# A fused attention, Fourier and MLP kernel whose tile scheduler orders the engines by its detailed timeline model

## The chip, the core and the metric

The kernel runs on one core of one Trainium2 chip. The metric is the device time of one execution in microseconds. Before the change the median of three runs is 1428.55 us (1426.3 to 1429.79).

## The reference

What is computed, for 8 batches, 8 heads, 576 positions, head size 64 (model width 512, MLP width 2048):

```
cum    = cumsum(max(s, 0))
scores = q @ k.T / 8 + min(-(cum_i - cum_j), 0), causal
attn   = softmax(scores)             # divided by (sum + 1e-9)
x      = attn @ v                    # heads side by side: 8 x 576 x 512
mixed  = real(fft(fft(x, axis=1), axis=2))
u      = x + mixed
un     = (u - mean(u)) / sqrt(var(u) + 1e-6)
out    = u + relu(un @ w_ch1) @ w_ch2
```

## The kernel before

Attention runs over 32 head pairs, one loop iteration i each. Every product that must be exact is made of a high and a low part. For pair i the iteration computes the scores (`scores`, L479): a multiplication of the high parts (L491) and one of the low parts q1 and k1 (L492), then an exponential on ScalarE (L495, output P) and a causal mask on GpSimd (L498, L501). Other pairs are at other stages in the same iteration:

- `load(i+3)` brings q and k from HBM (L403, tile qk).
- `high(i+2)` copies the high parts into one of three buffers KQ (L418, L420), with rows for the bias (L414, L416).
- `low(i+1)` moves halves of KQ to other partitions by DMA (L430, L431), subtracts on VectorE for k1 (L435) and on GpSimd for q1 (L438), and loads v (L441, tile va).
- `maxes(i+1)` multiplies high parts once more (12 multiplications, L459, tile pm) so that VectorE can take the maximum of each score row (L466; L462 for the first piece of a long row). The maxima (tile Mx) are transposed on TensorE (L471, pmt), copied (L473, mt) and written into KQ by DMA (L474): `scores` of that pair need that row.
- `av(i-1)` multiplies P with v (L523); ScalarE copies the result out (tile stage, L527 and L529) and the sums of the rows go out by DMA (L532).
- `recip(i-2)` takes the reciprocal of the sums (VectorE L538, L539), writes it to HBM (L541, rd) and reads it back spread over partitions (L544, rb). `finish(i-2)` multiplies on GpSimd (L559) into xa, or into xr, which three DMAs (L561 to L563) move into xs.

Tiles pm, pmt and the outputs of `av` share five PSUM banks.

Each batch has four pairs. When its xa and xs are there, `folds` (L244 to L267) adds and subtracts them: on VectorE Aw (L251), Df (L256, L260), low parts (L70) and e (L263 to L266), on GpSimd Bw (L253). This is called in iterations with i % 4 = 2 and 3; `fourier` of that batch follows over the next iterations. Its results are added to xa and xs (L322 to L325) and stored (uD, L327 to L329).

Beside this, `convert_w` turns 24 chunks of the weights from 64-bit to 32-bit floats: SyncE loads a chunk (L78, tile raw, 256 KB, one buffer), VectorE works on it (L83, L85, L88, L87), ScalarE (L84) and GpSimd (L89, tile we) too, and SyncE stores it (L98, wD). The rest of the weights is rounded after attention in `load_w`. Then come layer norm (`ln_tile`) and the MLP in 9 tiles of 512 tokens (`mlp_tile`).

The function `weave` interleaves these streams by weights and so gives the text one order. In the attention loop TensorE keeps it:

```
order.enter_context(tc.manual_schedule(engines={mybir.EngineType.PE}))
```

All other engines, and TensorE outside the loop, take their instructions in an order that the tile scheduler of the language chooses when the kernel is built. On the chip, each engine, and SyncE as issuer of DMAs, then runs its list strictly in that order; an instruction that waits holds everything behind it.

## Time and profile before

| | us |
|---|---|
| median of the runs | 1428.55 |
| profiled execution, its own time | 1426.1 |
| its span, first to last instruction | 1424.4 |
| TensorE busy in the span | 1305.1 |
| VectorE / ScalarE / GpSimd busy | 745.7 / 539.3 / 561.6 |
| TensorE idle from 700 us to 1424 us | 5.2 |
| TensorE idle ahead of 700 us | 114 |

The mean granted TensorE clock is 0.971 of full speed. Attention lasts to about 520 us, its last pairs, the last Fourier part and the first weights to about 700 us, and the MLP fills the rest. The profile's rows name tiles without their numbers, and "a<-b" reads "a is made from b". Times are counted from the start of the span. What stands in square brackets at the end of an instruction's row is the idle time of its engine ahead of it and what ended it.

### The profile page before, as it was taken

To read this page: it belongs to the slowest core of one execution; us is meant where nothing else is said; L and a number is where in the kernel's file an instruction comes from. 1 tells how busy PE (TensorE), PEld (TensorE's weight loads), DVE (VectorE), ACT (ScalarE), POOL (GpSimd) and SP (SyncE) were. 2 spreads that over 40 slices of the span, in tenths; PEclk is the share of its full clock that TensorE was granted. 3 is DMA by queue.
4 is the path that set the end of the run, shared out by engine and by line. 5 is a ranking of instruction groups with operands and counts; after the bars stand their busy time and mean duration, and the time that the engine had idled before them with its cause. 6 is when DMAs were issued, how large, how long until landed. Compare 5 with 4: busy or idle time off the path is not lost.

```text
span 1424.4 us, 17997 instructions
## 1 busy us (share of the span) xinstructions
PE 1305.1 (92%) x6190; PEld 1068.7 (75%) x6190; DVE 745.7 (52%) x1684; ACT 539.3 (38%) x1211; POOL 561.6 (39%) x543
## 2 busy tenths in 40 slices
PE   4887979897988887997899999999999999999998
PEld 3766868686777676775688888888888888888886
DVE  6667677877777788799833233222332223322212
ACT  4775756676665656344321121211212112121110
POOL 6445465656546566565720402204022040123300
PEclk9998999999999997999899999999999999999999
DMA  8555556565655555433200000000000000000000
GB/s 214 156 159 144 163 149 180 158 168 159 159 161 144 166 149 163 162 123 121 79 8 30 31 30 15 15 30 31 30 15 15 30 30 30 15 16 0 30 0 30
DMA packets 78230, 125.05 MB, mean 88 GB/s; under 512 B 11256, under 2 KB 36249, under 8 KB 78139
## 3 DMA queue, kind: packets, MB, share of 16 engines
q1 hardware_dynamic: 75627, 119.83, 28.4%
q0 software_dynamic: 1696, 2.50, 0.9%
q10 hardware_dynamic: 816, 1.57, 0.3%
q8 instruction: 49, 0.80, 0.2%
q14 instruction: 42, 0.34, 0.1%
HBM read 76.85 MB, written 23.07 MB: 70 GB/s over the span
## 4 chain that ended last, share of the span: by engine, by line
PE 51%; DVE 7%; POOL 2%; DMA 1%; issue 1%; ACT 1%; SPq 0%; DVEq 0%; POOLq 0%; ACTq 0%
PE h L183 25%; PE acc L198 8%; PE acc L196 8%; PE acc L197 8%; POOL we L89 1%; DVE wm L88 1%; DVE we L83 1%; DVE wm L85 1%; DVE we L87 1%; DVE wl L114 1%; ACT wh L112 1%; DMA wl<-wD 0%; POOL wl L114 0%; DVE ucl L148 0%; DVE zl L188 0%
## 5 line engine op out<-in xcount | busy, mean ns | idle before, releaser
L188 DVE SCALAR_TENSOR_TENSOR zl<-h,zh 128x512 fp32r<-128x512 f32 x144 | 98.6, 686 | 405.5 <-ACT zh L187 405.4
L187 ACT ACTIVATE zh<-h 128x512 fp32r<-128x512 f32 x144 | 85.9, 596 | 530.1 <-PE h L183 530.1
L198 PE MATMUL acc<-zl,wh 128*128 128x512 f32 x576 | 227.5, 396 | 4.9 <-DVE zl L188 4.9
L196 PE MATMUL acc<-zh,wh 128*128 128x512 f32 x576 | 227.6, 395 | 1.0 <-ACT zh L187 1.0
L197 PE MATMUL acc<-zh,wl 128*128 128x512 f32 x576 | 226.8, 394 | 0.0
L523 PE MATMUL pavB<-P,va 128*128 128x320 f32 (+2 forms) x640 | 189.1, 389 | 9.5 <-ACT stage L527 8.9
L459 PE MATMUL pm<-KQ 128*128 128x256 f32 (+3 forms) x384 | 156.5, 427 | 44.4 <-DVE Mx L466 23.1
L495 ACT ACTIVATE P<-ps 128x320 f32<-128x320 f32 (+4 forms) x384 | 145.9, 393 | 110.5 <-PE ps L492 106.8
L491 PE MATMUL ps<-KQ 128*128 128x256 f32 (+2 forms) x384 | 154.1, 404 | 24.4 <-ACT P L495 14.0
L183 PE MATMUL h<-uch,wh 128*128 128x512 f32 x576 | 159.9, 398 | 8.3 <-ACT wh L112 8.3
L183 PE MATMUL h<-uch,wl 128*128 128x512 f32 x576 | 158.1, 396 | 0.8 <-DVE wl L114 0.8
L183 PE MATMUL h<-ucl,wh 128*128 128x512 f32 x576 | 156.9, 393 | 0.0
L466 DVE CUSTOM_DVE_ANT_0 trash<-pm,amask 128x128 bf16<-128x128 f32 (+3 forms) x256 | 123.5, 482 | 34.2 <-PE pm L459 16.9
L212 POOL TENSOR_TENSOR o<-o,w 128x512 f32<-128x512 f32 x32 | 41.8, 1305 | 252.3 <-issue 218.5
L183 PEld LDWEIGHTS h<-uch,wh 128*128 128x128 f32 x576 | 108.2, 190 | 35.9 <-ACT wh L112 12.1
L198 PEld LDWEIGHTS acc<-zl,wh 128*128 128x128 f32 x576 | 108.7, 189 | 32.0 <-DVE zl L188 6.9
L183 PEld LDWEIGHTS h<-uch,wl 128*128 128x128 f32 x576 | 109.2, 190 | 26.6 <-DVE wl L114 1.2
L196 PEld LDWEIGHTS acc<-zh,wh 128*128 128x128 f32 x576 | 108.6, 188 | 26.1 <-ACT zh L187 1.8
L183 PEld LDWEIGHTS h<-ucl,wh 128*128 128x128 f32 x576 | 108.9, 189 | 24.7
L197 PEld LDWEIGHTS acc<-zh,wl 128*128 128x128 f32 x576 | 108.6, 189 | 24.7
L459 PEld LDWEIGHTS pm<-KQ 128*128 128x128 f32 x384 | 78.4, 207 | 64.7 <-DVE Mx L466 30.2
L492 PE MATMUL ps<-q,k 128*128 128x256 f32 (+2 forms) x384 | 120.5, 316 | 3.1 <-POOL q L438 3.1
(140 smaller groups left out, 2066.9 us busy)
## 6 DMA issues: line engine op xcount, KB each, us to landing
qk<-in_qkT_dram SPq DMA_DIRECT2D x32, 576.0 KB
raw<-in_wP_dram SPq DMA_DIRECT2D x64, 256.0 KB
va<-in_vA_dram SPq DMA_DIRECT2D x32, 480.0 KB
q<-KQ SPq DMA_DIRECT2D x32, 288.0 KB
k<-KQ SPq DMA_DIRECT2D x32, 288.0 KB
rb<-rd SPq DMA_DIRECT2D x64, 144.0 KB
u<-uD SPq DMA_DIRECT2D x8, 1024.0 KB
out_dram<-o SPq DMA_DIRECT2D x32, 256.0 KB
```

The lines of the kernel that those rows point to most:

```text
L183: nc.tensor.matmul(h[:, :n], a[:, j * 128:(j + 1) * 128], b[:, j, :n], start=i == 0, stop=i == 11)
L187: nc.scalar.activation(zh[:, :n], h[:, :n], AF.Relu)
L188: nc.vector.scalar_tensor_tensor(out=zl[:, :n], in0=h[:, :n], scalar=0.0, in1=zh[:, :n].bitcast(F32), op0=ALU.max, op1=ALU.subtract)
L196: nc.tensor.matmul(acc[j][:, :n], a[:, cs], y[:, :n], start=g == 0, stop=False)
L197: nc.tensor.matmul(acc[j][:, :n], b[:, cs], y[:, :n], start=False, stop=False)
L198: nc.tensor.matmul(acc[j][:, :n], a[:, cs], z[:, :n], start=False, stop=g == NF - 1)
L459: nc.tensor.matmul(p[:, :n], qy[:, h, 128 * c:128 * c + 128], ky[:, h, k0:k0 + n], start=True, stop=True)
L466: nc.vector.tensor_tensor_reduce(out=trash[:nq, :n], in0=p[:nq, :n], in1=amask[:nq, m0:m0 + n], scale=1.0, scalar=first if x else NEG, op0 ...
L491: nc.tensor.matmul(p[:, :n], ky[:, h, ksl], qy[:, h, a:a + n], start=True, stop=False)
L492: nc.tensor.matmul(p[:, :n], k1[:, h, ksl], q1[:, h, a:a + n], start=False, stop=True)
L495: nc.scalar.activation(P[:, o:o + a + n - lo], p[:, lo - a:n], AF.Exp, scale=0.125)
L523: nc.tensor.matmul(p[:, a - lo:n], va[:, c, vs], P[:, o:o + w], start=c == 0, stop=c == cs[-1])
```

## The change

One argument of the context in which the kernel is built:

```diff
-    with tile.TileContext(nc) as tc:
+    with tile.TileContext(nc, schedule_with_timeline_sim=True) as tc:
         fused_kernel(tc, *args)
```

The scheduler then chooses the order of the engines by a detailed model of their timelines instead of its plain one. The instructions are the same on every engine; their order is another. TensorE's order in the attention loop is written by hand and stays. On VectorE nearly every row has another place, on SyncE five of six.

The first place is VectorE in a fold iteration, around the k1 subtraction for pair 15. (k_2698 is that pair's k1, Mx_128 and Mx_129 are the maxima of pairs 14 and 15, KQ_119 to KQ_121 the three buffers.) Before:

```order
L466 ISA trash,Mx_128<-pm,amask,M_2491 64x320
L435 TENSOR_TENSOR k_2698<-qk,KQ_119 64x576 x2
L466 ISA trash,Mx_129<-pm,amask 128x128
L83 TENSOR_SCALAR we<-raw 128x256
...
L538 TENSOR_SCALAR sums<-sums 32x36
L539 RECIPROCAL sums<-sums 32x36
...
L251 TENSOR_TENSOR Aw<-xa,xs 128x576
L466 ISA trash,Mx_129<-pm,amask 128x512
```

After the change:

```order
L466 ISA trash,Mx_128<-pm,amask,M_2491 64x320
L466 ISA Mx_128 64x1
L251 TENSOR_TENSOR Aw<-xa,xs 128x576
L263 TENSOR_TENSOR e<-xs 1x288
L264 COPY e<-xs 1x1
L435 TENSOR_TENSOR k_2698<-qk,KQ_119 64x576
L256 TENSOR_TENSOR Df<-Aw 128x289
L435 TENSOR_TENSOR k_2698<-qk,KQ_119 64x576
L251 TENSOR_TENSOR Aw<-xa,xs 128x576
L466 ISA trash,Mx_129<-pm,amask 128x128
```

The first folds moved ahead of k1 and of all maxima of pair 15; the conversion that stood there (L83) is done earlier. It is so for batches 1 to 6.

The second place is SyncE in the same iteration. Before:

```order
L541 DMA rd<-sums 32x36
L532 DMA sums<-stage 16x1x36
L474 DMA KQ_121<-mt 1x10x128
L544 DMA rb<-rd 64x576 x2
L441 DMA va<-in_vA_dram 128x5x192
L532 DMA sums<-rows 16x1x36
L403 DMA qk<-in_qkT_dram 128x1152
L561 DMA xs<-xr 112x576
L562 DMA xs<-xr 15x576
L563 DMA xs<-xr 1x16x36
```

After the change:

```order
L541 DMA rd<-sums 32x36
L544 DMA rb<-rd 64x576 x2
L403 DMA qk<-in_qkT_dram 128x1152
L561 DMA xs<-xr 112x576
L532 DMA sums<-stage 16x1x36
L562 DMA xs<-xr 15x576
L563 DMA xs<-xr 1x16x36
L98 DMA wD<-we 128x256
L474 DMA KQ_121<-mt 1x10x128
```

The stores to xs moved ahead of the row of maxima (L474) and of the loads that were between them and rb.

The third place is SyncE in the start, around the rows of maxima of pairs 0 and 1 (into KQ_119 and KQ_120). Before:

```order
L414 DMA KQ_120<-cumhl 2x1x576 x2
L441 DMA va<-in_vA_dram 128x5x192
L474 DMA KQ_119<-mt 1x10x128
L430 DMA q_220<-KQ_120 64x2x576
L431 DMA k_221<-KQ_120 64x2x576
L414 DMA KQ_121<-cumhl 2x1x576 x2
L441 DMA va<-in_vA_dram 128x5x192
L474 DMA KQ_120<-mt 1x10x128
```

After the change:

```order
L414 DMA KQ_121<-cumhl 2x1x576 x2
L441 DMA va<-in_vA_dram 128x5x192
L78 DMA raw<-in_wP_dram 128x512
L403 DMA qk<-in_qkT_dram 128x1152
L78 DMA raw<-in_wP_dram 128x512
L474 DMA KQ_119<-mt 1x10x128
L403 DMA qk<-in_qkT_dram 128x1152
L98 DMA wD<-we 128x256
L78 DMA raw<-in_wP_dram 128x512
L98 DMA wD<-we 128x256
L474 DMA KQ_120<-mt 1x10x128
```

Loads and stores of `convert_w` (L78, L98) moved ahead of both rows of maxima. Over the whole attention loop, all 24 chunks stand ahead of the k1 of pair 15 on VectorE; before, 9 did, and 20 stood ahead of the last k1.

## The prediction

> **What bounds the kernel now.** I read the engine shares of the page first, then a table of stretches, then what TensorE and VectorE waited for in attention, and last single instructions. The first row says that TensorE (PE) is the bound; the columns of the second fence are the stretch, its length, and the busy time and (instructions) of each engine, then the granted clock, the DMA share and GB/s.
>
> ```profile
> PE 1305.1 (92%) x6190; PEld 1068.7 (75%) x6190; DVE 745.7 (52%) x1684; ACT 539.3 (38%) x1211; POOL 561.6 (39%) x543
> ```
>
> ```profile
> 0.00:60.00 60.00, 38.34 (x164) 29.87 (x164) 39.30 (x120) 30.95 (x66) 31.74 (x45) 0.94 0.78 195
> 60.00:520.00 460.00, 397.99 (x2254) 336.54 (x2255) 336.92 (x970) 294.66 (x733) 261.01 (x270) 0.96 0.56 157
> 520.00:700.00 180.00, 149.97 (x670) 118.01 (x669) 158.88 (x322) 87.90 (x200) 111.90 (x113) 0.92 0.41 133
> 700.00:1424.00 724.00, 718.77 (x3108) 584.33 (x3106) 210.54 (x275) 125.82 (x214) 156.98 (x116) 1.00 0.07 24
> ```
>
> From 700 us on, the MLP, TensorE is idle 724.00 - 718.77 = 5.2 us: nothing to win there. Ahead of it TensorE is idle 21.7 us in the start, 62.0 us in attention and 30.0 us in the tail of attention and first weights. Only these 114 us can shrink; they can grow without limit. The next rows (engine and line waited for: total, times, longest) show that the 62 us of attention are many short waits, and that VectorE (DVE) itself idles 51.9 us for the release of k1.
>
> ```profile
> PE pm L459 <- DVE Mx L466: 22.4, 11, 5.5
> PE ps L491 <- ACT P L495: 11.0, 15, 2.2
> DVE k L435 <- PE ps L492: 51.9, 19, 4.6
> DVE sums L538 <- DMA sums<-rows: 5.8, 6, 2.7
> ```
>
> TensorE's biggest wait is for VectorE reading score maxima (L466) out of the five banks, and it comes where the folds of L251 to L266 sit in one burst. So the change is judged by where it puts VectorE's folds and conversions, and by what SyncE (SP) has queued ahead of the transfers that VectorE then waits for.
>
> **Folds ahead of k1 (second place of the order).** In the changed order, in six fold iterations (batches 1 to 6), Aw and e, which need xs, stand ahead of the two k1 subtractions and of the first maxima of the next pair; before, they stood behind eight reads of maxima. VectorE stops at Aw until xs has landed. The same iteration in the trace (start, duration, engine, line, the idle before):
>
> ```profile
> 223.83 2.30 DVE L435 TENSOR_TENSOR k<-qk,KQ 64x576 fp32r<-64x576 f32 x2
> 230.60 0.37 DVE L539 RECIPROCAL sums<-sums 32x36 f32<-32x36 f32 x1
> 236.90 0.40 SPq L541 DMA_DIRECT2D rd<-sums  x1
> 239.42 1.86 DVE L435 TENSOR_TENSOR k<-qk,KQ 64x576 fp32r<-64x576 f32 x2 [4.00 <-PE ps L492]
> 239.77 1.15 SPq L544 DMA_DIRECT2D rb<-rd  x2
> 244.07 1.42 POOL L559 TENSOR_TENSOR xr<-stage,rb 128x576 f32<-128x576 f32 x1 [0.43 <-DMA rb<-rd]
> 245.52 0.56 SPq L561 DMA_DIRECT2D xs<-xr  x1
> 247.04 0.55 SPq L563 DMA_DIRECT2D xs<-xr  x1
> 249.92 0.79 DVE L251 TENSOR_TENSOR Aw<-xa,xs 128x576 f32<-128x576 f32 x1
> ```
>
> ```profile
> 579.75 0.54 SPq L563 DMA_DIRECT2D xs<-xr  x1
> 581.62 1.94 POOL L253 TENSOR_TENSOR Bw<-xa,xs 128x576 f32<-128x576 f32 x1 [4.65 <-DMA xs<-xr]
> L263 DVE TENSOR_TENSOR e<-xs 1x288 f32<-1x288 f32 x6 | 7.5, 1258 | 0.0
> ```
>
> Suppose SP issues rd the moment the reciprocals end, at 230.60 + 0.37 = 230.97; before, older rows of the queue held it to 236.90. Then: rd to rb 239.77 - 236.90 = 2.87; rb to xr 244.07 - 239.77 = 4.30; xr to its first store 1.45; first to last store issue 1.52; last store to use 581.62 - 579.75 = 1.87; one stage load more between the stores, about 0.6 by their spacing. Sum 12.6, so xs is there at about 243.6, while k1 started at 239.42: VectorE would stand 4.2 us. With Aw 0.79 and e 1.26 ahead of it, k1 and the maxima start 6.2 us later. TensorE's order is fixed, and five banks cover it for a while: an iteration, 239.42 - 223.83 = 15.6 us from k1 to k1, uses 17 of them (12 maxima, 4 av, 1 mt), so five are worth at most 15.6 * 5 / 17 = 4.6 us. Queued behind the waiting Aw are k1, wanted one iteration later, and the maxima, wanted at once; so TensorE loses 1.6 to 6.2 us per batch. In return the burst is gone from the next iteration, and with it the 22.4 us of waits for Mx, 3.3 per batch over about 6.8 batches. Net -1.7 to +2.9 by these; since SP also has the mt row (L474) behind the xs stores, which stops scores by itself, I take +2 per batch, times six = **+12** (bounds: all waits gained and none paid, -20; 6.2 - 3.3 and the mt row later by another stall's 0.6, +21).
>
> A rule beside it: the Trainium skill, "TensorE: Matmul & The Clock Gate", Part 1 on the HAM clock gate, has the clock fall to half after an idle window of about 3.4 us. Here two stretches with a wait for Mx in them show the granted clock:
>
> ```profile
> 129.56 0.69 PE L459 MATMUL pm<-KQ 128*128 128x384 f32 x1 [2.60 <-DVE Mx L466]
> 196.87 0.69 PE L459 MATMUL pm<-KQ 128*128 128x384 f32 x1 [4.30 <-DVE Mx L466]
> 125.00:133.00 8.00, 4.75 (x12) 3.52 (x13) 5.92 (x16) 3.37 (x9) 4.00 (x5) 0.50 0.82 231
> 195.00:203.00 8.00, 4.89 (x15) 3.63 (x16) 5.82 (x17) 3.15 (x8) 3.80 (x5) 0.57 0.80 267
> ```
>
> The clock is 0.50 and 0.57 against 0.96 over attention: 4.89 us of work at 0.57 would take 4.89 * 0.57 / 0.96 = 2.9, so such a stall costs 2 us more than itself. By the page only stalls of 3.4 us and more do that, so six new long ones would add 12 us and the sum would rise to 1456; the trace halves the clock after a wait of 2.60 as well, so old stalls paid the same, and I put the exchange at 0.
>
> **Conversions early (third place, the start).** All 24 chunks are converted ahead of the k1 of pair 15, instead of 9, and none in the last iterations. One costs VectorE, by the rows of attention (count, then busy, mean ns):
>
> ```profile
> L83 DVE TENSOR_SCALAR we<-raw 128x256 int32<-128x256 int32 x18 | 8.3, 462 | 0.3 <-DMA raw<-in_wP_dram 0.3
> L88 DVE SCALAR_TENSOR_TENSOR wm<-raw,wm 128x256 f32<-128x256 uint16 x18 | 7.6, 423 | 0.5
> L87 DVE SCALAR_TENSOR_TENSOR we<-raw,we 128x256 int32<-128x256 int32 x18 | 7.6, 422 | 0.0
> L85 DVE TENSOR_SCALAR wm<-raw 128x256 int32<-128x256 int32 x18 | 6.4, 354 | 0.0
> ```
>
> That is 1.66 us, 15 chunks moved = 25 us of work, hidden in the 123 us that VectorE idles in attention; uncovered it costs 25. But raw is one buffer, so each load waits on SP until the chunk before is converted, with everything behind it. Where VectorE reaches a chunk early, it pays part of the landing: 0.3 us in all before, at most 546.41 to 551.83 = 5.4 us each in the fence below. I take 0.2 for each of 15 = **+3** (0 to +11, an estimate of 0.7 each).
>
> The start is where this shows. The second raw load now stands on SP ahead of the first mt row (L474), so that row waits for the first chunk to land and be converted.
>
> ```profile
> 16.03 1.36 SPq L414 DMA_DIRECT2D KQ<-cumhl  x2
> 21.19 0.84 SPq L474 DMA_DIRECT2D KQ<-mt  x1
> 29.70 0.81 SPq L474 DMA_DIRECT2D KQ<-mt  x1
> 36.91 0.55 PE L491 MATMUL ps<-KQ 128*128 128x256 f32 x1 [3.63 <-DMA KQ<-mt]
> 546.41 0.37 SPq L78 DMA_DIRECT2D raw<-in_wP_dram  x1
> 551.83 0.29 DVE L83 TENSOR_SCALAR we<-raw 128x256 int32<-128x256 int32 x1 [1.29 <-DMA raw<-in_wP_dram]
> ```
>
> With the rows of KQ at 16.03 as before and nine issues of some 0.65 us to the raw load: 21.8. Landing 5.4 later: 27.2. Conversion and the second load: 28.9; the first mt row at 29 in place of 21.19, and scores of pair 0 some 6 to 8 us late. The second mt row stands behind another chunk, 5.4 + 1.7 later: 36 instead of 29.70; but then it needs less than the 7.2 us (36.91 - 29.70) that it took among the table loads. I take **+5** for the start, +2 to +9.
>
> **The tail.** Four chunks (24 against 20 by the last k1) leave it, and the second half of the last rb no longer waits behind the stores of uD:
>
> ```profile
> 567.33 1.17 POOL L89 TENSOR_TENSOR we<-wm,we 128x256 f32<-128x256 f32 x1
> 568.53 0.34 SPq L98 DMA_DIRECT2D wD<-we  x1
> 568.91 0.45 SPq L544 DMA_DIRECT2D rb<-rd  x1
> 573.95 0.33 SPq L328 DMA_DIRECT2D uD<-xs  x1
> 574.33 0.49 SPq L544 DMA_DIRECT2D rb<-rd  x1
> ```
>
> That half waited 574.33 - 568.91 = 5.4 us and the first one on a store of wD, itself behind GpSimd's L89. Against it the last rd now stands behind the xs stores of the pair ahead. The rounding that follows is bound by VectorE, so what the last batch gains reaches the end. I take **-4** (-10, both rows and two chunks; 0, all given back).
>
> MLP: same work in nearly the same order, TensorE idle 5.2 us in all: 0.
>
> **Sum.** 12 + 3 + 5 - 4 = +16 on the span of 1424.4 = 1440.4; the profiled execution's own time, 1426.1, gives 1442.1; the median of the runs lies 2.45 above it, so **1444.5**.
>
> **Rivals.** (1) xs is there in time: the spread folds end TensorE's waits for Mx, -20, tail -10, start +3 and no landing paid: -27, **1401**. For it: 22.4 us of waits have that cause, and rb, xs and the stage copies come earlier on their queues. Against it: the 12.6 us after the reciprocals are transfers and one multiplication, which no order shortens. It decides if VectorE reaches Aw later than 243.6 in the count above, that is if its own iteration is 4 us slower or recip 4 us earlier.
> (2) SP's queue becomes the bound: 24 chunks, each with a load and a store that wait there in order, hold transfers back by 2 us each: +48, **1476**. For it: in the tail the rb row stood behind such a store (568.53), which stood behind GpSimd's L89 (567.33 + 1.17); the 2 us are an estimate from that. Against: in attention 18 chunks in the same queue cost VectorE 0.3 us of waits for raw, and most such waits hide.
> (3) Stalls and gains meet: folds 0, start and landing 8, tail and Mx -8: **1428**; any sum between -4 and +4.
> That the change moves nothing is excluded by the order, which differs in nearly every row of VectorE and SP.
>
> **How the numbers follow.** Forecast 0.48, rival (1) 0.30, (2) 0.10, (3) 0.12. Slower by over 0.3% (4.3 us, about what a measurement of this kernel can tell from no change): 0.48 + 0.10 = 0.58; within it 0.12; faster 0.30. The bounds of the terms add up to -20 + 0 + 2 - 10 = -28 and 21 + 11 + 9 + 0 = +41, on 1428.55: 1401 to 1470. That is the range: it ends at rival (1)'s own time and short of rival (2)'s. The forecast's own range, where its terms don't all go one way, is 1433 to 1462.
>
> **What would show it.** Right: waits of VectorE at Aw or e for xs, 3 to 6 us in six iterations; k1's wait for ps (51.9) much smaller; the first score multiplication after 30 us; the last wD store before 300 us; waits of TensorE for Mx not under 22 us. Wrong: Aw without a wait and Mx waits under 10 us (rival 1), or attention longer with SP waiting on conversions (rival 2), or a tail (520 to 700) that grows.

## The result and the profile after

The changed kernel takes 1506.46 us (median of three, 1506.32 to 1506.78) against 1428.55: 1.0552 times as long, 95% interval 1.0531 to 1.0572. The forecast was 1444.5 with a range to 1470. The sign was right, and the loss, 78 us, is five times the 16 forecast and lies outside the range.

The profiled execution has a span of 1504.8 us, 80.4 more than before. First the busy times by engine and then the table of stretches of the changed kernel, the last two cut 80 us later than before (columns as there):

```profile
PE 1334.2 (89%) x6190; PEld 1088.8 (72%) x6190; DVE 735.1 (49%) x1684; ACT 538.8 (36%) x1211; POOL 555.8 (37%) x543
```

```profile
0.00:60.00 60.00, 29.91 (x129) 22.82 (x129) 35.53 (x111) 28.92 (x61) 31.51 (x46) 0.97 0.79 201
60.00:600.00 540.00, 434.66 (x2276) 362.69 (x2274) 355.61 (x991) 299.91 (x744) 261.22 (x274) 0.91 0.50 137
600.00:780.00 180.00, 152.37 (x680) 119.82 (x681) 139.91 (x308) 83.93 (x192) 102.34 (x104) 0.91 0.37 127
780.00:1504.00 724.00, 717.31 (x3109) 583.42 (x3108) 204.06 (x276) 126.07 (x216) 160.77 (x121) 1.00 0.06 22
```

Nearly all of it is in attention: 540 us for about the work that took 460. The last two stretches hold the work of before, 680 and 3109 multiplications against 670 and 3108, in the same time. TensorE is busy 1334.2 - 1305.1 = 29.1 us more for the same 6190 multiplications, and most of that is the granted clock, 0.91 in attention and not 0.96: summed over slices of 1 us, busy time times granted clock is 1272.7 before and 1277.0 now, so 25 of the 29 us are clock. The other 51 us are more idle time, 540.00 - 434.66 = 105.3 in attention against 62.0.

The first and the last k1 row mark where the time is lost. Before and after, from the timeline of VectorE (start, duration, engine, line, the idle before):

```profile
48.69 1.86 DVE L435 TENSOR_TENSOR k<-qk,KQ 64x576 fp32r<-64x576 f32 x2 [2.21 <-PE ps L492]
511.61 1.86 DVE L435 TENSOR_TENSOR k<-qk,KQ 64x576 fp32r<-64x576 f32 x2 [3.79 <-PE ps L492]
```

```profile
55.92 1.43 DVE L435 TENSOR_TENSOR k<-qk,KQ 64x576 fp32r<-64x576 f32 x2 [1.75 <-PE ps L492]
591.00 1.43 DVE L435 TENSOR_TENSOR k<-qk,KQ 64x576 fp32r<-64x576 f32 x2
```

The first pair is the k1 of pair 3, the second the last k1. The changed kernel is 7.2 us late at pair 3, 41.7 at pair 15 (281.12 against 239.42), 79.4 at the last and 80.4 at the end of the span. So the start costs 7, attention 72, and tail and MLP 1. Of the 72, 34 come up to pair 15, where weights are converted, and 38 after it, where none are left.

What the engines waited for in attention (60 to 600 us): total, times, longest. First TensorE, then VectorE, then SyncE as issuer:

```profile
PE pm L459 <- DVE Mx L466: 64.5, 39, 4.6
PE ps L491 <- ACT P L495: 16.0, 9, 3.6
PE ps L491 <- DMA KQ<-mt: 0.8, 2, 0.5
```

```profile
DVE sums L538 <- DMA sums<-rows: 41.4, 18, 4.1
DVE k L435 <- PE ps L492: 25.7, 16, 4.0
DVE Aw L251 <- issue: 15.2, 3, 5.4
DVE Aw L251 <- DMA xs<-xr: 11.1, 3, 5.6
DVE wm L85 <- DMA raw<-in_wP_dram: 9.0, 6, 2.7
DVE we L83 <- DMA raw<-in_wP_dram: 7.8, 2, 3.9
```

```profile
SPq L541 <- DMA sums<-rows: 54.2, 23, 4.5
SPq L541 <- DVE Mx L466: 33.0, 16, 4.8
SPq L541 <- DVE sums L539: 19.6, 9, 4.9
SPq L544 <- DMA rd<-sums: 19.0, 23, 3.0
SPq L98 <- POOL we L89: 1.1, 3, 0.4
```

("issue" stands where the profile names nothing that was waited for.) The rows of before that these and later ones are held against (60 to 520 us):

```profile
SPq L544 <- DMA rd<-sums: 11.2, 11, 2.6
SPq L541 <- DVE Mx L466: 2.8, 8, 0.5
```

```profile
PE ps L491 <- DMA KQ<-mt: 3.1, 6, 0.8
```

Before, the row of 2.8 us is SyncE's longest at L541 (the store of rd), and the others there are under 1 us each; now three rows add up to 107. All of SyncE's waits together are 326 of 540 us, 216 of 460 before. TensorE's wait for maxima is three times as long, and VectorE, which must produce them, waits in its own order for the sums of rows (L538: 41.4, 5.8 before). One iteration shows the chain. Changed kernel, SyncE's timeline, with VectorE's row at the sums between:

```profile
241.79 0.60 SPq L532 DMA_DIRECT2D sums<-rows  x1
242.44 0.93 SPq L431 DMA_DIRECT2D k<-KQ  x1
243.46 0.55 SPq L78 DMA_DIRECT2D raw<-in_wP_dram  x1
249.49 0.34 SPq L541 DMA_DIRECT2D rd<-sums  x1
250.90 1.12 SPq L544 DMA_DIRECT2D rb<-rd  x2
```

```profile
247.39 1.32 DVE L538 TENSOR_SCALAR sums<-sums 32x36 f32<-32x36 f32 x1 [2.91 <-DMA sums<-rows]
```

The sums are issued at 241.79 and used on VectorE at 247.39, after it stood 2.91 us. The order has rd as the third DMA behind the sums, so SyncE issues nothing from 243.46 + 0.55 = 244.0 to 249.49, and nothing again until rd has landed for rb. In the iteration of before that the prediction follows, the sums went out here:

```profile
225.02 0.56 SPq L532 DMA_DIRECT2D sums<-rows  x1
```

Their rd came at 236.90, ten other DMAs later, and between rd and rb stood a copy of sums and the row of maxima. The new order puts sums, reciprocal, rd and rb close behind one another, as if each transfer landed when it is wanted. It is so without conversions too. The changed kernel's SyncE, between two neighbours of its list:

```profile
399.08 0.98 SPq L431 DMA_DIRECT2D k<-KQ  x1
405.86 0.33 SPq L541 DMA_DIRECT2D rd<-sums  x1
```

For 405.86 - 400.06 = 5.8 us nothing is issued.

### The profile page after: what moved, and what is told of

Same layout as the page of the kernel before. It is cut to its first block, busy times and chain, and to the rows that moved or that the text cites. A ratio compares the mean times of both kernels' runs of the same rounds, so it can differ in the third digit from the quotient of the medians.

```text
span 1504.8 us, 18038 instructions
## 1 busy us (share of the span) xinstructions
PE 1334.2 (89%) x6190; PEld 1088.8 (72%) x6190; DVE 735.1 (49%) x1684; ACT 538.8 (36%) x1211; POOL 555.8 (37%) x543
## 4 chain that ended last, share of the span: by engine, by line
PE 49%; DVE 6%; DMA 2%; issue 1%; POOL 1%; ACT 1%; SPq 0%; DVEq 0%; POOLq 0%; ACTq 0%
PE h L183 24%; PE acc L196 8%; PE acc L198 8%; PE acc L197 8%; DMA raw<-in_wP_dram 1%; DVE wm L85 1%; DVE wl L114 1%; DVE we L87 1%; DVE we L83 1%; POOL we L89 1%; DVE wm L88 0%; DMA u<-uD 0%; DVE ucl L148 0%; DMA wl<-wD 0%; DVE zl L188 0%
## 5 line engine op out<-in xcount | busy, mean ns | idle before, releaser
L459 PE MATMUL pm<-KQ 128*128 128x256 f32 (+3 forms) x384 | 160.2, 434 | 86.7 <-DVE Mx L466 66.1
L198 PE MATMUL acc<-zl,wh 128*128 128x512 f32 x576 | 215.7, 396 | 2.1 <-DVE zl L188 2.1
L523 PE MATMUL pavB<-P,va 128*128 128x320 f32 (+2 forms) x640 | 196.5, 402 | 4.1 <-DVE Mx L466 2.6
L491 PE MATMUL ps<-KQ 128*128 128x256 f32 (+2 forms) x384 | 162.6, 426 | 30.4 <-ACT P L495 16.9
L438 POOL TENSOR_TENSOR q<-qk,q 64x576 fp32r<-64x576 f32 x64 | 91.2, 1444 | 102.7 <-DMA q<-KQ 70.6
```

Of the source, the lines that this page charges most:

```text
L198: nc.tensor.matmul(acc[j][:, :n], a[:, cs], z[:, :n], start=False, stop=g == NF - 1)
L438: nc.gpsimd.tensor_sub(q1[64:128, h], qk[0:64, h], q1[0:64, h].bitcast(F32))
L459: nc.tensor.matmul(p[:, :n], qy[:, h, 128 * c:128 * c + 128], ky[:, h, k0:k0 + n], start=True, stop=True)
L491: nc.tensor.matmul(p[:, :n], ky[:, h, ksl], qy[:, h, a:a + n], start=True, stop=False)
L523: nc.tensor.matmul(p[:, a - lo:n], va[:, c, vs], P[:, o:o + w], start=c == 0, stop=c == cs[-1])
```

## The experiments

Nearly all hold an engine to a listed order of the same instructions, by edges that carry no wait of their own. An order is that of the kernel before ("old"), of the changed one, or one of them with rows moved. What is not held is ordered by the scheduler with its timeline model around it. No run holds the changed orders without a move; but in the trace of "Sums ahead of the v loads" TensorE, VectorE and ScalarE run the lines of the changed kernel in the same order. The edit, once:

```diff
+def _pin(tc, engine, packed, first, last):
+    names = ...    # the listed instructions
+    for a, b in zip(names, names[1:]):
+        tc.add_manual_dep(have[b], a, DependencyInfo(NoSync, DATA), reason="pin")
...
     with tile.TileContext(nc, schedule_with_timeline_sim=True) as tc:
         fused_kernel(tc, *args)
+        _pin(tc, mybir.EngineType.DVE, ORDER0, 0, None)
```

Where an expectation names a theory by a letter, V is that VectorE's own order makes the loss, and L that transfers land after they are asked for, so that cures for single landings add up. In each median below, the ratio is to the kernel before on the same chip, with its 95% interval.

### Taking single stalls out of the changed kernel

**Reciprocals later.** The changed orders are held; in 30 pairs L538 and L539 stand two reads of maxima later on VectorE.

```diff
-L538 TENSOR_SCALAR sums<-sums 32x36
 L466 ISA trash,Mx_129<-pm,amask,M_510 64x320
-L539 RECIPROCAL sums<-sums 32x36
 L466 ISA trash,Mx_129<-pm,amask 128x128
+L538 TENSOR_SCALAR sums<-sums 32x36
 L466 ISA trash,Mx_129<-pm,amask 128x256
+L539 RECIPROCAL sums<-sums 32x36
```

> The changed kernel with the order of every engine held as it was built, and on VectorE alone the reciprocals of the row sums (L538, L539) of 30 pairs each two reads of maxima later. Theory V (VectorE's new order is the cause: it stops at instructions that stand ahead of the landing of their data, and TensorE pays through the banks of maxima): VectorE's wait at L538 falls from about 50 us to under 25, TensorE's wait for maxima from 66 us to about 45, the time from 1506 to 1480-1490. Theory S (SyncE's new order makes the sums, xs and mt rows late for everybody): the wait moves to another instruction, 1500-1510.

1511.03 us, 1.0565 [1.0529, 1.0602]: nothing is won, against theory V. The waits of VectorE and of TensorE in this kernel (60 to 600 us):

```profile
DVE sums L538 <- DMA sums<-rows: 9.5, 9, 3.9
PE pm L459 <- DVE Mx L466: 21.1, 21, 2.8
PE ps L491 <- ACT P L495: 40.1, 23, 3.6
```

The stall for the sums is gone (41.4 to 9.5), and TensorE's wait for maxima with it, back to the level of before. But TensorE now waits 40.1 us for P instead of 16.0. VectorE's stall was a place where lateness showed; an account that fits, not shown, is that the chain behind the reciprocals came later by what VectorE won.

**Folds later.** The changed orders of TensorE, GpSimd and SyncE are held and so is VectorE's with the folds of batches 1 to 6 seven reads of maxima later; ScalarE follows.

```diff
+L466 ISA trash,Mx_129<-pm,amask 128x384
...
+L466 ISA trash,Mx_129<-pm,amask 128x128
 L251 TENSOR_TENSOR Aw<-xa,xs 128x576
 L263 TENSOR_TENSOR e<-xs 1x288
```

> The changed kernel with TensorE, GpSimd and SyncE held as built, and on VectorE the 13 fold instructions (L251 to L266) of batches 1 to 6 each seven reads of maxima later; ScalarE is ordered anew to fit. Theory V: VectorE's wait of 26 us at Aw for xs goes to under 5, k1 and the maxima of six pairs start 5 to 7 us sooner, the time falls by 20 to 35 us to 1471-1486; by the prediction's price of a stall (about 6 us each less what is hidden), by 10 to 25. Theory S: less than 8 us of change, since the mt row stays behind the xs stores.

1516.03 us, 1.0597 [1.0556, 1.0637]: no gain either. VectorE's wait at Aw is gone, the one for the sums has grown:

```profile
DVE Aw L251 <- DMA xs<-xr: 0.4, 1, 0.4
DVE sums L538 <- DMA sums<-rows: 50.8, 21, 4.9
```

TensorE's wait for maxima stays at 60.7, 64.5 in the changed kernel. So the stall that the prediction made its largest term was there and gave nothing back when it was taken away.

**Sums ahead of the v loads.** The changed orders are held; on SyncE 29 loads of v (480 KB each) stand behind the next sums.

```diff
-L441 DMA va<-in_vA_dram 128x5x192
 L532 DMA sums<-rows 16x1x36
+L441 DMA va<-in_vA_dram 128x5x192
```

> The changed kernel with the order of every engine held as built, and on SyncE alone each load of v (L441, 480 KB) that stood just ahead of the load of the row sums (L532 from rows) put behind it, 29 times. Theory S: the sums land 1 to 3 us sooner, VectorE's wait at L538 falls from about 50 us to 20 or less, 1470-1485. Theory V: the sums are copied out too late for VectorE's place of the reciprocals whatever SyncE does, the wait falls by 10 to 20 us, 1490-1503.

1489.34 us, 1.0419 [1.037, 1.0468]: 0.0133 * 1428.55 = 19 us less than the changed kernel, just short of the gain that theory S forecast. The wait for the sums is gone on VectorE, and part of TensorE's waits has moved on to P (25.6):

```profile
DVE sums L538 <- DMA sums<-rows: 1.8, 2, 0.9
PE pm L459 <- DVE Mx L466: 23.7, 22, 3.2
PE ps L491 <- ACT P L495: 25.6, 12, 5.1
```

Here landing earlier helps; waiting later, in the two runs before, did not.

**Both, and the copies too.** As the last one, with the reciprocals of the first and the ScalarE copy L527 next to the second copy, 31 times.

```diff
 # DVE as in "Reciprocals later", SP as in "Sums ahead of the v loads", ACT:
-L527 COPY stage<-pavA 64x256
 ...
 L529 COPY stage<-pavB 128x320
+L527 COPY stage<-pavA 64x256
```

> The changed kernel with every engine's order held as built, and three things that hang on the row sums moved: the 29 loads of v behind the load of the sums on SyncE, the reciprocals two reads later on VectorE, and ScalarE's first copy of the second head to stage (L527) next to the second one. Theory L (the order reckons with transfers that land sooner than they do, and its consumers stop at them on every engine): the gains add up, 1506 to 1455-1475. Theory J (any mixture of orders is as slow): 1485-1500, no better than the loads of v alone.

1494.49 us, 1.0462 [1.0438, 1.0486]: no better than the v loads alone. TensorE's waits now appear at the row of maxima (60 to 560 us):

```profile
PE ps L491 <- DMA KQ<-mt: 26.1, 11, 5.9
```

The three cures of the sums do not add up, against theory L. For other landings it is not tested: VectorE still waits 40.0 us for raw and 39.1 at Aw in this kernel (60 to 600 us).

### Which engine's order it is

**One engine old, the others by the model.** Five kernels: VectorE; SyncE; ScalarE; SyncE and ScalarE; VectorE and SyncE.

```diff
+        _pin(tc, mybir.EngineType.DVE, ORDER0, 0, None)         # first
+        _pin(tc, mybir.EngineType.SP, ORDER0, 0, None)          # second
+        _pin(tc, mybir.EngineType.Activation, ORDER0, 0, None)  # third; fourth: SP and Activation; fifth: DVE and SP
```

> The detailed timeline model orders all engines but VectorE, which is held in the order that it had before the change (TensorE by hand as always). Theory V: VectorE's order alone brings back most of it, 1425-1450. Theory S, or a cause on ScalarE and GpSimd: SyncE's queue still holds back what VectorE waits for, 1470-1500.

> The detailed model orders all engines but SyncE, which is held in the order that it had before the change. Theory Q (the order of the DMA queue on SyncE is the cause: sums, xs and mt rows come late, and ScalarE's copy to stage at L527 waits for the load of the sums that stands far back there): 1430-1455, and ScalarE's wait at L527 for sums<-stage goes from 32 us to under 5. Theory A (ScalarE's order is the cause: copies of KQ, L418, and of stage ahead of their time hold back exponentials and the sums behind them): 1485-1505, the waits of VectorE for sums stay over 30 us. Theory J (each engine's new order only fits the others' old ones, any mixture is slow): over 1500.

> The detailed model orders all engines but ScalarE, which is held in its order of before. Theory A: 1430-1455, TensorE's waits for maxima and for exponentials both near those of before (23 and 14 us). Theory Q: 1485-1505, ScalarE's wait at L527 for sums<-stage stays or moves to the next copy. Theory J: over 1500.

> SyncE and ScalarE both held in their orders of before, VectorE and GpSimd ordered by the detailed model. If VectorE's new order costs nothing by itself (as its old order among the others' new ones brought nothing back): 1425-1440. If VectorE's folds ahead of k1 cost what was predicted, about 2 us in each of six batches and a start some 5 us later: 1440-1455. Theory J: over 1480.

> VectorE and SyncE both held in their orders of before, ScalarE and GpSimd ordered by the detailed model. Theory Q: 1425-1440. Theory A: 1465-1500 with TensorE waiting for ScalarE's P or stage. Theory J: over 1480.

| old | us | ratio | less than changed, us |
|---|---|---|---|
| VectorE | 1502.72 | 1.0513 [1.048, 1.0545] | 6 |
| SyncE | 1485.16 | 1.0395 [1.0359, 1.0431] | 22 |
| ScalarE | 1494.89 | 1.0476 [1.0427, 1.0524] | 11 |
| SyncE and ScalarE | 1462.25 | 1.0244 [1.0209, 1.0279] | 44 |
| VectorE and SyncE | 1479.9 | 1.0371 [1.0324, 1.0418] | 26 |

(The last column is the difference of the ratios to 1.0552, times 1428.55.) Theory V falls: VectorE's old order returns 6 of 78 us, and its interval overlaps that of the changed kernel. Neither SyncE nor ScalarE brings back by itself what theories Q and A wanted, 1430 to 1455. The two together return 44, the sum of the two alone is 33; the difference is about the size of the noise.

These kernels undo more than the list that they hold. In all five the model put the conversions back to about their old places: 9 or 10 chunks stand ahead of the k1 of pair 15, not 24. Counted along each list in the traces, the lists that it formed stand 1 to 4 places from the old ones on average, and on VectorE 34 to 36 places from that of the changed kernel. (There four rows in five have another place than before, which is less than "nearly every row".) With VectorE's own order old, the folds too stand where they stood before. Still 73 us are lost, and as early as in the changed kernel. The k1 of pair 15 in that run:

```profile
282.39 1.43 DVE L435 TENSOR_TENSOR k<-qk,KQ 64x576 fp32r<-64x576 f32 x2 [6.72 <-PE ps L492]
```

That is 43.0 us late; pair 3, at 58.01, is 9.3 late. Between them lie 34 us, as in the changed kernel, though 9 chunks are converted by then and not 24. So neither early conversions nor the folds are needed for the loss; moves of a few places on SyncE, ScalarE and GpSimd are enough.

**One engine new, the other three old.** With a control in which all four are old, and only TensorE outside the loop is ordered by the model. In these the model orders the free engine around three held lists, so its order is not that of the changed kernel: on average its rows stand 1 to 3 places from the old order, and 36 (VectorE), 23 (SyncE), 12 (ScalarE) and 9 (GpSimd) places from the changed one. The conversions stay at about their old places. "New" means the model's own small moves here.

```diff
+        _pin(tc, mybir.EngineType.DVE, ORDER0, 0, None)         # left out where VectorE is new
+        _pin(tc, mybir.EngineType.SP, ORDER1, 0, None)          # left out where SyncE is new
+        _pin(tc, mybir.EngineType.Activation, ORDER2, 0, None)  # left out where ScalarE is new
+        _pin(tc, mybir.EngineType.Pool, ORDER3, 0, None)        # left out where GpSimd is new
```

> All four, VectorE, SyncE, ScalarE and GpSimd, held in their orders of before; the detailed model orders only TensorE outside the attention loop. If the loss lies in the orders of these four, and holding an order costs nothing: 1424-1432, no difference from before. If TensorE's own changed places (first maxima, MLP) matter: above 1435.

> SyncE, ScalarE and GpSimd held in their orders of before; the detailed model orders VectorE (and TensorE outside the attention loop) around them. By the prediction's terms for VectorE alone (folds ahead of k1 +12, start up to +5) 1435-1450. If what was left with SyncE and ScalarE held (+35 us) came from GpSimd's new order: 1425-1432. If VectorE's new order only costs where others are late too: 1425-1435.

> VectorE, ScalarE and GpSimd held in their orders of before; the detailed model orders SyncE around them. If SyncE's new order costs by itself what holding it brought back (20 to 30 us): 1445-1460. If it only costs together with the others' new orders: 1425-1435, and VectorE waits less than 12 us for sums.

> VectorE, SyncE and GpSimd held in their orders of before, the detailed model orders ScalarE around them. If the loss is a sum of what each engine's new order costs by itself: about 78 - 5 - 17 - 30 = 26 us remain for ScalarE and GpSimd together, so 1435-1455 here. If ScalarE only loses by others' lateness: 1428-1436.

> VectorE, SyncE and ScalarE held in their orders of before, the detailed model orders GpSimd around them. With VectorE and GpSimd new 35 us were lost, with VectorE alone new 21: so 12 to 15 us for GpSimd if they add, 1440-1450; 1428-1436 if GpSimd loses only by VectorE's lateness.

| new | us | ratio | net of the control, us |
|---|---|---|---|
| none (control) | 1435.01 | 1.0032 [1.0013, 1.005] | |
| VectorE | 1447.41 | 1.015 [1.0115, 1.0186] | 17 |
| SyncE | 1465.21 | 1.0244 [1.0198, 1.0289] | 30 |
| ScalarE | 1469.98 | 1.0293 [1.0266, 1.032] | 37 |
| GpSimd | 1440.47 | 1.008 [1.0053, 1.0107] | 7 |

Each new order loses by itself, ScalarE's and SyncE's most; GpSimd's 7 is barely outside the noise. The four add up to 91. The changed kernel loses 74 beside the control, but with other orders, so the one doesn't check the other. Where VectorE alone is new, its attention is only 7.8 us later at the last k1 (control -2.5) and the rest is lost in the tail; and its Aw has no waits to speak of, since the folds there kept about their old places; so this run doesn't size them either. Where ScalarE alone is new, TensorE waits for P and ScalarE for q and k (60 to 560 us):

```profile
PE ps L491 <- ACT P L495: 32.4, 21, 4.0
ACT KQ L418 <- DMA qk<-in_qkT_dram: 26.3, 10, 4.6
```

ScalarE's exponentials stand behind a copy (L418) that waits for its load, and TensorE behind the exponentials (6.9 and 11.0 before). Where SyncE alone is new, it stands at rb:

```profile
SPq L544 <- DMA rd<-sums: 39.4, 22, 4.6
```

### One move of SyncE alone

**rb directly behind rd.** All four old orders; in 32 pairs the two loads of rb stand directly behind rd. Before, one to three rows stood between; in the changed kernel none does in 14 pairs, and one in 14 others.

```diff
 L541 DMA rd<-sums 32x36
-L474 DMA KQ_120<-mt 1x10x128
 L544 DMA rb<-rd 64x576 x2
+L474 DMA KQ_120<-mt 1x10x128
 L532 DMA sums<-rows 16x1x36
```

> VectorE, ScalarE and GpSimd held in their orders of before, SyncE too but for one thing: the two loads of rb (L544) stand directly behind the write of rd (L541) for all 32 pairs, as in the changed order, ahead of the rows of maxima (L474) and sums that stood between. Theory R (SyncE stands at rb for the trip of rd, over 2 us an iteration, and holds the mt row and the sums back): SyncE's wait at L544 for rd goes from 12 us to about 40, 1440-1465. Otherwise (xr and xs come sooner, the wait hides): 1420-1432.

1468.21 us, 1.0278 [1.0237, 1.032], net of the control 0.0246 * 1428.55 = 35 us for the move of 64 loads by a row or a few. SyncE's and TensorE's waits (60 to 520 us) say how:

```profile
SPq L544 <- DMA rd<-sums: 61.4, 26, 5.4
PE ps L491 <- DMA KQ<-mt: 37.9, 15, 4.4
```

SyncE stands 61.4 us for rd's trip to HBM, 11.2 before, and the row of maxima, now behind it, reaches the scores late: 37.9 against 3.1. That wait has grown by 35 us, as much as the kernel, but the match is partly chance: TensorE is also busy 15.5 us more than in the control (1321.7 against 1306.2), and waits less for maxima (9.1, 22.4 before). The Trainium skill, "DMA: Bandwidth & Descriptors", Anatomy of one DMA (told there for the GpSimd path), says that a semaphore wait is made on the issuing sequencer ahead of dispatch; these two rows agree, and show its price for what is queued behind. The price is not that of the changed kernel, where SyncE stands 19.0 us at rb and TensorE waits 0.8 for the row of maxima: there SyncE's standing is at rd.

### The conversions alone

**Converted early.** The plain scheduler of before and one line changed, so that all 24 chunks stand ahead of the k1 of pair 14. The scheduler forms its orders anew around that.

```diff
-        share = NC1 * 4.0 / (NP - 2) if i < NP - 2 else (1.0, 4.0)[i - NP]
+        share = 1.65
-    with tile.TileContext(nc, schedule_with_timeline_sim=True) as tc:
+    with tile.TileContext(nc) as tc:
```

> The kernel of before, ordered by the plain scheduler, with one line changed: 1.65 chunks of weights are converted per iteration instead of 0.6, so that all 24 are done ahead of the k1 of pair 14. By the prediction's terms: conversions +3 (0 to +11), tail without four chunks -4 (-10 to 0): 1420-1436. If early conversions and their loads are the cause of the slower iterations: 1445 or more, with the loss in the first 14 iterations.

1479.97 us, 1.0368 [1.0336, 1.0401]: 52 us. The k1 of pairs 3, 7, 11 and 15 are 1.6, 23.5, 41.9 and 57.3 us late, those of pairs 19 and 23 58.3 and 59: (57.3 - 1.6) / 12 = 4.6 us an iteration while chunks are converted and next to nothing after. The stretch from 60 to 250 us and waits in it, before, then here:

```profile
60.00:250.00 190.00, 162.36 (x907) 136.78 (x908) 136.72 (x396) 124.46 (x308) 103.29 (x108) 0.95 0.57 158
SPq L98 <- POOL we L89: 2.6, 2, 1.5
```

```profile
60.00:250.00 190.00, 138.53 (x660) 115.87 (x660) 119.61 (x348) 99.07 (x243) 88.92 (x92) 0.84 0.49 139
SPq L98 <- POOL we L89: 52.7, 14, 8.8
DVE we L83 <- DMA raw<-in_wP_dram: 27.6, 7, 4.4
ACT we L84 <- DVE we L83: 35.6, 13, 5.3
```

VectorE is less busy, not more, as less gets done in the stretch (660 multiplications, 907 before). SyncE stands 52.7 us at the store of wD (L98, 2.6 before) until GpSimd has made the chunk, VectorE 27.6 for the next load of raw, which is queued behind that store, and ScalarE 35.6 for VectorE. TensorE's clock falls to 0.84. In the changed kernel, with the same 24 chunks early, the first of these waits is 1.1 us and VectorE's for raw 9.0 + 7.8; so the run shows what early conversions can cost, and not what they cost there.

**The store on another queue.** The same, with the store of wD issued by GpSimd, which makes the chunk.

```diff
-                nc.sync.dma_start(out=wD[f, :, WC * x:WC * x + WC], in_=m)
+                nc.gpsimd.dma_start(out=wD[f, :, WC * x:WC * x + WC], in_=m)
```

> As the run with 1.65 chunks per iteration (e20, 1480 us), with one line more: the store of wD (L98) is issued by GpSimd, which makes its data, instead of SyncE. Theory W (SyncE's standing at the store is the cause): at least half of the 52 us come back, 1430-1455. Rival (the conversion's work and its waits on VectorE and ScalarE cost by themselves, 36 us at raw and 44 us at L84): 1465-1485.

1464.5 us, 1.0227 [1.021, 1.0245]: 20 of the 52 us come back, with all orders formed anew once more. SyncE no longer stands at the store, but it now stands at the next load of raw until VectorE is done with the buffer (60 to 250 us; this row was 2.1 in the run before):

```profile
SPq L78 <- DVE Mx L466: 30.8, 12, 8.5
```

Another 8.6 us at that load are put down to L87. VectorE still waits 24.2 us for the next chunk, and ScalarE 36.1 for VectorE. So the move took the standing at the store away and much of it came back at the load; the rest is not divided further.

**The xs stores on another queue.** The kernel before, with the three stores to xs issued by GpSimd, to see whether relief for SyncE wins anything.

```diff
-            nc.sync.dma_start(out=xs[1:113, j - 2], in_=dst[0:112])
+            nc.gpsimd.dma_start(out=xs[1:113, j - 2], in_=dst[0:112])
 ...             # L562 and L563 alike
```

> The kernel of before with one edit: the three stores to xs (L561 to L563) are issued by GpSimd, which makes xr, instead of SyncE, so SyncE no longer stands 33 us for xr and issues some 45 DMAs less. If SyncE's standing bounds attention already before: 1400-1424. If the fixed order of TensorE and the folds are the bound there: 1424-1433. If GpSimd's issues hold back its mask and q1 work: 1433-1450.

1462.32 us, 1.0218 [1.0198, 1.0237]: slower, and above all three forecasts. VectorE waits at Aw for xs as in the changed kernel (18.7 us), and ScalarE for q and k (29.2).

The plain scheduler put all engines in a new order around this edit too, so the run doesn't tell the queue from the order. It shows no gain from relieving SyncE of these stores; why it is slower stays open.

No kernel here beats the one before.

## Why the prediction was right in sign and wrong in size

**The step that failed: what the sum left out.** It priced the folds and conversions of VectorE, the start and the tail. The new order of sums, rd and rb on SyncE, and the whole lists of ScalarE and GpSimd, stood in it at nothing, without a reason. The runs show the reverse: with VectorE's old order held, folds and conversions are back in place, and 73 of the 78 us stay lost; small moves on SyncE alone cost 30 us, on ScalarE alone 37. So the right sign was largely luck: the folds and conversions that gave the forecast its sign return 6 us when they are undone.

**Folds ahead of k1 (+12 of 16).** The stall came as told: VectorE stands at Aw in five of the six iterations, for 4.5 to 5.6 us, where 4.2 were worked out. One of them:

```profile
278.69 0.76 DVE L251 TENSOR_TENSOR Aw<-xa,xs 128x576 f32<-128x576 f32 x1 [4.93 <-DMA xs<-xr]
```

Its wait for the release of k1 shrank from 51.9 to 25.7, and TensorE's waits for maxima are not under 22.4 but 64.5. The cost is not shown: taking the stall away returned nothing. The term took a stall that ends in a wait of TensorE for a loss of that length. In this loop another late chain stands ready right behind: the sums when the folds were moved, P or the row of maxima when the sums were.

**Conversions early (+3, bounds 0 to +11): too low, but not what the loss needs.** It priced a chunk as 1.66 us of VectorE that hides in idle time and 0.2 of waiting for raw, with 25 us as the price uncovered. In attention of the changed kernel VectorE waits 9.0 + 7.8 = 16.8 us for raw, over the bound of 11. In the kernel converted early by the plain scheduler 52 us are lost, so the 25 was no bound: a chunk occupies more than VectorE, as the waits at L98, L84 and raw show there. The text saw that "each load waits on SP until the chunk before is converted, with everything behind it", and then took 0.2 us each from a row in which the chunks were spread out. But the 52 can't be carried over. SyncE's wait at the store of wD, 52.7 us there, is 1.1 in the changed kernel, and the loss up to pair 15 is the same 34 us with the chunks back.

**rb close behind rd: left out of the sum.** The second place of the order showed it, and the working used it only for how early xs would be there; rival (1) even counted it as a gain. Alone, in 32 pairs, it costs 35 us. The prediction asked when rb arrives, and not what waits behind it on SyncE. In the changed kernel the same kind of standing is found one row earlier: 107 us at rd.

**ScalarE and GpSimd: not looked at.** Small new orders of theirs alone cost 37 and 7 us. The part on the change speaks of VectorE and SyncE only.

**Start (+5, +2 to +9): right in size, in part by luck.** 7.2 us at pair 3; the first score multiplication of the changed kernel starts at 35.29 us, past the 30 named, and the last store of wD is issued at 277.58, before 300. The second load of raw did stand ahead of the first mt row (31.93 and 32.35, where 29 was worked out). But the working kept the rows of KQ where they were, and TensorE's first multiplication of all, which waits for such a row, starts at 18.61 us and not at 11.70. With VectorE's old order, where a single load of raw stands ahead of the first mt row (26.34), pair 3 is 9.3 us late all the same.

**Tail (-4) and MLP (0).** From the last k1 to the end it is 80.4 - 79.4 = 1 us more: the gain of four chunks didn't reach the end. The MLP idles 6.7 us, 5.2 before.

**The clock (0).** This was a choice against the sum of 1456, and wrong: TensorE is busy 29.1 us more, over a third of the loss. The prediction exchanged old stalls for new ones, but there are more of them, 39 waits for maxima where there were 11; the granted clock is under 0.75 in 93 of the 540 slices of 1 us in attention, 42 of 460 before. Nor does the trace show that the wait of 2.60 us halved the clock. That wait ran from 126.96 to 129.56, and the clock was down before it:

```profile
124.00:125.00 1.00, 0.55 (x1) 0.29 (x1) 1.00 (x1) 0.00 (x0) 1.00 (x1) 0.50 0.00 0
```

It fell between 123 and 124 us, in the second of two waits of 2.68 and 0.85 us with one multiplication between them. The Trainium skill, "TensorE: Matmul & The Clock Gate", Part 1 on the HAM clock gate, lets the clock fall after idle time of some 3.4 us; the trace agrees in the sign (0.96 to 0.91 over attention), and the waits for maxima that go with it are 4.6 us at the longest.

**The rivals.** (1), faster, fell with the first wait at Aw. (2), SyncE's queue as the bound, came nearest (1476, chance 0.10): attention longer, with SyncE standing, was its sign. But it had SyncE standing for the conversions alone, and in attention of the changed kernel SyncE waits 1.1 us for GpSimd's part of a chunk (L98); it stands most at rd, for the sums and for VectorE, also where no chunk is left (405.86 above). So its nearness in time is luck.

**What stays open.** How the 78 us divide, and which moves on SyncE and ScalarE make the most of them. Alone, the four engines' small new orders cost 91, and old orders given back one by one return 6, 11 and 22. No single move explains it, and the runs show no first cause among them. What early conversions cost in the changed kernel itself is not shown: no run there moves them alone. Also open: the other three fifths of their cost under the plain scheduler, and the slower run with the xs stores on GpSimd.

## What to carry to other kernels

Price a reordering on every engine that runs its list in order, the issuer of DMAs first, and don't pass over small moves: here places changed by 1 to 4 were enough. For each row that moved ask what it waits for there and what is queued behind it, not when its own result is wanted. A step that passes over several queues costs what it holds up on each of them, so its busy time on one engine is no upper bound. And when one stall in such a loop is taken away, look where the wait goes before counting a gain: of the single stalls taken away here, only that where the data landed earlier won time.

## What was not expected of the hardware

Dependent transfers placed next to one another on one issuing queue, in 32 pairs, cost 2.5% of the kernel, though SyncE waits no more than 5.4 us at any of them (61.4 in all). And VectorE read the sums 247.39 - 241.79 = 5.6 us after their last transfer of 16 * 36 floats was issued, having waited for it, while transfers moved 137 GB/s on average over attention. Last, about 25 of the 80 us are a lower clock: with many waits for maxima of at most 4.6 us goes a granted clock of 0.91 over attention, 0.96 before.
